# Turning the exponentials and outputs of a local and global attention block on VectorE, with products in 32x32 tiles

## The chip, the cores and the metric

The kernel runs on one core of one Trainium2 chip. The metric is device time in microseconds of one launch. A core has TensorE (matrix products, into PSUM, eight banks of 128 partitions by 512 fp32), VectorE (DVE), ScalarE (ACT), GpSimd (POOL) and a queue engine SP that only issues transfers. Every engine runs its own queue in order and waits on semaphores.

## The reference

Attention over 8 batches and 8 heads of dimension 64, with 512 local and 32 global positions, followed by one wide gated layer, called the mixture of experts (MoE) below.

```python
k_all = np.concatenate([k_g, k_l], axis=2)
s_g = scale * np.matmul(q_g, k_all.transpose(0, 1, 3, 2))
out_g = np.matmul(sm(s_g), v_all)
mask = np.abs(pos[:, None] - pos[None, :]) <= 32
s_ll = np.where(mask, scale * q_l @ k_l.T, -1e9)
s_l = np.concatenate([scale * q_l @ k_g.T, s_ll], axis=-1)
out_l = np.matmul(sm(s_l), np.concatenate([v_g, v_l], axis=2))
x = concatenate([out_g, out_l])        # (4352, 512)
h = x @ w_in                           # (512, 2048)
return (h * np.clip(h + 3, 0, 6) / 6) @ w_out
```

`sm` is a softmax with the row maximum taken off. A local query sees the 32 global keys and local keys at most 32 positions away.

## The kernel before

Positions are cut in 16 blocks of 32. A block of 32 queries sees three blocks of keys (its own and the two beside it) and the 32 global keys, 128 keys in all. A *unit* is one call of `local(b, j, q)`: 128 queries (four blocks) and four of the eight heads, so there are 8 units a batch and 64 in all.

`quad_qk` turns queries and keys on TensorE (L390) and copies them out of PSUM to `qt` and `kt` (L224 on ScalarE, L226 on VectorE). A unit then runs: scores (16 products with 96 local keys, L416, and 16 with 32 global keys, L417); per head, VectorE adds the mask and takes the maximum (L428, written as two instructions); ScalarE takes the exponential into `ex` (L434). `ex` has queries on partitions and must be turned before it can multiply V. For batches 0 to 2 TensorE turns it through PSUM (L446, copied by L224 or L226); for batches 3 to 7 a DMA transpose issued on the SP queue does (L439). Then 16 products with V (L453), one per head and block of queries, each 128 keys by 32 queries, go to the bank `a`, and VectorE divides by the sums (L462, L463) into `x`. `x` is turned again for the MoE: by TensorE for batch 0 (L477), by DMA for the others (L484).

V needs, for each block of queries, its 128 keys on the 128 partitions: the tile `vs` holds one such column of blocks for each of the 16 blocks. It is loaded from memory in part and copied within the chip in part; for batches 0 and 1 TensorE makes it with products with a 0/1 matrix (`pick`, L317), and the global V is spread by GpSimd (L305). `globe` does the 32 global queries of four heads at a time (L501 to L544) and spreads their output over `xg` (L548 to L558).

The MoE: `first` makes 128 hidden features for up to 512 tokens (L582, four products), ScalarE and VectorE apply the gate (L588, L590); `second` makes 128 tokens of the output from 16 products (L601), copied out by L608 or L610 and stored by SP.

The order of each queue is laid beforehand by `Plan.lay`, a list scheduler over named streams with ranks: each `Op` has costs in microseconds per engine, a latency and buffers that it takes and reads. Buffers come from pools of a given size (`sizes`). TensorE's filler is the stream `moe`; attention units of batch b are spread over the MoE of batch b - 1 by `hold`. PSUM is used as: three banks `m` for MoE, two for `s` (two slots of scores), two `t` for turns, one `a`.

Of the kernel before, what the change touches and what calls it, by code (L numbers as in the profile page):

```python
# [13 lines left out]
class Buf:  # L14


    __slots__ = ("pool", "slot", "left", "free_at")

    def __init__(self, pool, readers):
        self.pool, self.slot, self.left, self.free_at = pool, None, readers, 0.0  # L20
# [13 lines left out]
class Plan:  # L34
# [3 lines left out]
    def __init__(self, pools):  # L38
        self.free = {p: [0.0] * n for p, n in pools.items()}
        self.streams = {}  # L40
        self.rank = {}
# [9 lines left out]
    def ready(self, op):  # L51
        t = 0.0
        for d in op.deps:
            if d.end is None:
                return None
            t = max(t, d.end)
        need = {}
        for b in op.takes:
            need[b.pool] = need.get(b.pool, 0) + 1
        for p, n in need.items():  # L60
            slots = sorted(x for x in self.free[p] if x is not None)
            if len(slots) < n:
                return None
            t = max(t, slots[n - 1])
        return t

    def lay(self):
        at = {n: 0 for n in self.streams}
# [3 lines left out]
        while len(order) < total:  # L72
            found = []
            for n, ops in self.streams.items():
# [3 lines left out]
                t = self.ready(op)  # L78
# [12 lines left out]
            if len(op.on) > 1:  # L91
                start, end, e = min((f[0], f[2], f[4]) for f in found if f[3] == n)
                start, end, e = min(((f[0], f[2], f[4]) for f in found if f[3] == n), key=lambda f: f[1])
            at[n] += 1
            clock[e] = end
            op.end, op.engine = end + op.lat, e
            for b in op.takes:
                slots = [(x, i) for i, x in enumerate(self.free[b.pool]) if x is not None]
                b.slot = min(slots)[1]
                self.free[b.pool][b.slot] = None  # L100
            for b in op.reads:
                b.left -= 1
                b.free_at = max(b.free_at, op.end)
                if b.left == 0:
                    self.free[b.pool][b.slot] = b.free_at
# [5 lines left out]
def kernel(  # L111
# [22 lines left out]
    NT = Sl // P  # L134
    W = 32
    NU = P // W
    NB = Sl // W
    NQ = H // 4
    T = 8
    D1 = D + 2  # L140
    NC1 = (NB - 1) // 3
    NS = NB
    PERM = 2
# [12 lines left out]
    def tiles(name, n, shape, dtype, pool=None):  # L156
        return [(pool or sb).tile(shape, dtype, tag=f"{name}{i}", name=f"{name}{i}") for i in range(n)]

    sizes = {"nat": 2, "qkg": 1, "gT": 2, "kt": 2, "v": 2, "ex": 4, "sm": 8, "et": 5, "x": 3, "xt": 3,
             "xgn": 2, "t1": 3, "ot": 3, "m": 3, "s": 2, "t": 2, "a": 1, "eg": 2, "mx": 12, "rec": 4}  # L160
    for c in range(NDFF):
        sizes[f"gts{c}"] = 1

    qn = tiles("qn", 2, [P, NP, T * D], FP16)
    kn = tiles("kn", 2, [P, NP, T * D], FP16)
    qkg = tiles("qkg", 1, [P, H * D], FP16)
    gT = tiles("gT", 2, [P, NQ, 2, P], FP16)
    qt = [tiles(f"qt{r}_", NQ, [P, 2, Sl], FP16) for r in range(2)]
    kt = [tiles(f"kt{r}_", NQ, [P, 2, Sl + 2 * W], FP16) for r in range(2)]
    vs = tiles("vs", 2, [P, NS, H, D1], FP16)  # L170
    vraw = tiles("vraw", PERM, [P, H, NT * D], FP16)
    pick = tiles("pick", 1, [P, NT, Sl + 2 * W], FP16)[0]
    exs = tiles("ex", 4, [P, 4, P], FP16)
    sms = tiles("sm", 8, [P, P], FP32)
    ets = tiles("et", 5, [P, 6 * P], FP16)
    egs = tiles("eg", 2, [P, 6, P], FP16)
    xs = tiles("x", 3, [P, H, D], FP16)
    xts = tiles("xt", 3, [P, NP, Sl], FP16)
    xgns = tiles("xgn", 2, [P, 2, D], FP16)
    xg = tiles("xg", 1, [P, NP, B * Sg], FP16)[0]  # L180
# [3 lines left out]
    recs = tiles("rec", 4, [P, 4, 1], FP32)  # L184
    masks = tiles("mask", 3, [P, P], FP32)
    ident = tiles("ident", 1, [P, P], FP16)[0]
    w_in_t = tiles("win", 4, [P, NP, dff // 4], FP16)
# [4 lines left out]
    mps = tiles("m", 3, [P, 512], FP32, pp)  # L192
    sps = tiles("s", 1, [P, 2 * 512], FP32, pp)[0]
    tps = tiles("t", 2, [P, 1024], FP16, pp)
    aps = tiles("a", 1, [P, 4, D1], FP32, pp)

    plan = Plan(sizes)
    for name, rank in (("l0", 0), ("ld", 5), ("sh", 0), ("et", 0), ("tr", 0), ("st", 2),
                       ("gq", 3), ("gqc", 2), ("qt", 4), ("qtc", 3), ("kg", 1), ("pm", 2), ("pmc", 1), ("vb", 6),
                       ("s", 2), ("mx", 2), ("ex", 2), ("t", 1), ("etc", 2), ("av", 0), ("nm", 1),  # L200
                       ("xp", 1), ("xpc", 1), ("gx", 1), ("gxc", 1),
                       ("moe", 9), ("t1", 0), ("gate", 0), ("ot", 3)):
        plan.stream(name, rank)
    for name in ("l0", "ld", "sh", "et", "tr", "st"):
        plan.stream("dq" + name, 0 if name in ("l0", "ld") else -1)

    def load(stream, engine, issue, service, o, i, deps=(), takes=(), reads=(), transpose=False, lat=2.0):
        eng = {"POOL": nc.gpsimd, "SP": nc.sync}[engine]

        def emit():  # L210
            a, b = o() if callable(o) else o, i() if callable(i) else i
            if transpose:
                eng.dma_start_transpose(out=a, in_=b)
            else:
                eng.dma_start(out=a, in_=b)  # L215
# [17 lines left out]
    BY_DMA = range(3, B)  # L233

    def slot(i):
        return (2 * NC1, 0, NC1)[i % 3] + i // 3

    def setup():
        for r in range(2):
            nc.vector.memset(vs[r][0:W, slot(0), :, :], 0.0)  # L240
            nc.vector.memset(vs[r][2 * W:3 * W, slot(NB - 1), :, :], 0.0)
            nc.vector.memset(vs[r][:, :, :, D:D1], 1.0)
            nc.vector.memset(egs[r], 0.0)
            for q in range(NQ):
                nc.vector.memset(kt[r][q][:, :, 0:W], 0.0)
                nc.vector.memset(kt[r][q][:, :, W + Sl:], 0.0)

    def band():
        m = masks[1]
        nc.vector.memset(m, 0.0)  # L250
# [462 lines left out]
```

## Time and profile before

| | us |
|---|---|
| median of three runs | 400.56 (400.41 to 403.77) |
| the profiled execution | 400.83 |
| its span, first to last instruction | 399.1 |
| granted TensorE clock, mean | 0.987 |

In the profile PE is TensorE, PEld its weight loads, DVE VectorE, ACT ScalarE, POOL GpSimd. A group's line names line, engine, operation, output and inputs, shapes and count, then busy time, mean duration of one in ns, idle time of the engine just before them and what ended it. Products overlap, so their durations are not their pace: the time from one start to the next is.

```profile
L428 DVE CUSTOM_DVE_ANT_0 sm<-s,mask 128x128 f32<-128x128 f32 x256 | 61.8, 285 | 15.6 <-PE s L417 14.7
L453 PE MATMUL a<-vs,et 128*32 128x65 f16 x1024 | 20.1, 198 | 19.5 <-DMA et<-ex 19.5
L463 DVE TENSOR_TENSOR x<-a,rec 128x256 f16<-128x256 f32 x64 | 27.1, 424 | 2.2
```

For instance the last of these: 64 instructions on VectorE of 424 ns, each reading 128 partitions by 256 fp32 from the bank `a`.

### The profile page before, as it was taken

The page shows a single profiled execution, that of the slowest core. Times are in us where ns is not written, and L with a number is a line of the kernel's source. Part 1 is how long each engine was busy: PE and PEld are TensorE (multiplying, and loading weights), DVE is VectorE, ACT ScalarE, POOL GpSimd, SP SyncE. Part 2 cuts the span into 40 slices and gives each one's busy share as a digit, 9 for nine tenths or more (in the row PEclk, how much of TensorE's full clock was granted, in tenths as well). Part 3 has the DMA queues.
Part 4 walks back from the last instruction along what each step waited for, and adds up shares of the span by engine and source line. Part 5 has one row for each costly group of instructions (what it writes and reads, how often), then busy time and mean ns, then how long its engine had stood idle before and what let it go on. Part 6 is the DMA issues. An engine that isn't in the chain of part 4 may idle for free.

```text
span 399.1 us, 13569 instructions
## 1 busy us (share of the span) xinstructions
PE 352.7 (88%) x5604; PEld 181.4 (45%) x5604; DVE 269.5 (68%) x995; ACT 211.9 (53%) x504; POOL 130.4 (33%) x148
## 2 busy tenths in 40 slices
PE   2279899999899988998499987999889989999996
PEld 2245676645444533454234533454334434444562
DVE  5573898687998757876476765876875787457150
ACT  1066778635486456744465563755763576245251
POOL 8953309920880193008900193007400000000000
PEclk9999999999999999999879998999999999999999
DMA  8999929637993199439954299339554442310202
GB/s 109 202 207 207 213 42 113 142 87 151 114 194 58 52 174 206 62 94 120 161 99 102 81 150 206 71 85 119 131 80 107 95 41 53 82 53 2 79 3 79
DMA packets 92942, 44.15 MB, mean 111 GB/s; under 512 B 72176, under 2 KB 86992, under 8 KB 92880
## 3 DMA queue, kind: packets, MB, share of 16 engines
q0 software_dynamic: 48320, 17.77, 40.4%
q1 hardware_dynamic: 44560, 25.51, 31.6%
q8 instruction: 44, 0.72, 0.7%
q14 instruction: 18, 0.15, 0.1%
HBM read 35.52 MB, written 8.91 MB: 111 GB/s over the span
## 4 chain that ended last, share of the span: by engine, by line
PE 59%; DMA 18%; DVE 12%; ACT 4%; POOL 3%; issue 3%; SPq 0%; POOLq 0%; DVEq 0%; ACTq 0%
PE m L601 22%; PE m L582 19%; DMA et<-ex 17%; PE m L317 4%; PE a L453 3%; DVE sm L428 3%; PE s L416 2%; DVE qt L226 2%; ACT ex L434 2%; PE t L390 2%; DVE gts L590 1%; ACT t L588 1%; PE t L523 1%; DVE kt L226 1%; PE t L446 1%
## 5 line engine op out<-in xcount | busy, mean ns | idle before, releaser
L582 PE MATMUL m<-xt,win 128*128 128x512 f16 (+1 forms) x576 | 126.2, 364 | 2.4 <-DVE gts L590 1.8
L434 ACT ACTIVATE ex<-sm,mx 128x128 f16<-128x128 f32 x256 | 88.6, 392 | 65.4 <-DVE mx L428 65.0
L601 PE MATMUL m<-wout,gts 128*128 128x512 f16 x512 | 122.9, 380 | 0.0
L588 ACT ACTIVATE t<-m 128x512 f32<-128x512 f32 (+1 forms) x160 | 84.7, 532 | 44.8 <-PE m L582 38.4
L590 DVE SCALAR_TENSOR_TENSOR gts<-t,m 128x512 f16<-128x512 f32 (+1 forms) x144 | 88.9, 624 | 13.3 <-ACT t L588 12.4
L582 PEld LDWEIGHTS <-win 128*128 128x128 f16 x640 | 58.9, 99 | 54.9 <-issue 8.3
L428 DVE CUSTOM_DVE_ANT_0 sm<-s,mask 128x128 f32<-128x128 f32 x256 | 61.8, 285 | 15.6 <-PE s L417 14.7
L215 POOL DMA_DIRECT2D vs<-in_v_l_dram x42 | 29.8, 716 | 127.2 <-PE a L533 116.9
L601 PEld LDWEIGHTS <-gts 128*128 128x128 f16 x512 | 44.8, 98 | 50.1 <-issue 2.5
L305 POOL COPY vs<-vs 32x2640 f16<-32x2640 f16 x21 | 49.4, 2402 | 0.0
L462 DVE RECIPROCAL rec<-a 128x4 f32<-128x4 f32 x64 | 11.5, 180 | 40.3 <-PE a L453 40.1
L453 PE MATMUL a<-vs,et 128*32 128x65 f16 x1024 | 20.1, 198 | 19.5 <-DMA et<-ex 19.5
L608 ACT COPY ot<-m 128x512 f32<-128x512 f32 x22 | 12.9, 585 | 41.0 <-PE m L601 38.1
L453 PEld LDWEIGHTS <-et 128*32 128x32 f16 x1024 | 12.1, 97 | 45.7 <-DMA et<-ex 27.6
L416 PE MATMUL s<-kt,qt 64*32 64x96 f16 x1024 | 21.7, 211 | 11.3 <-DVE kt L226 6.8
L463 DVE TENSOR_TENSOR x<-a,rec 128x256 f16<-128x256 f32 x64 | 27.1, 424 | 2.2
L416 PEld LDWEIGHTS <-qt 64*32 64x32 f16 x1024 | 13.9, 93 | 19.2 <-issue 11.1
L226 DVE COPY et<-t 128x512 f16<-128x512 f16 (+1 forms) x30 | 14.2, 477 | 12.3 <-PE t L523 9.5
L226 DVE COPY qt<-t 128x1024 f16<-128x1024 f16 x16 | 19.5, 1221 | 2.9 <-PE t L390 2.5
L428 DVE DVE_READ_ACCUMULATOR2_ANT mx<- 128x1 f32 x256 | 21.2, 83 | 0.1
L513 ACT ACTIVATE eg<-s,mx 128x480 f16<-128x480 f32 x16 | 10.6, 661 | 19.3 <-DVE mx L508 17.6
L417 PE MATMUL s<-gT,qt 64*32 64x32 f16 x1024 | 19.5, 180 | 0.0
(73 smaller groups left out, 307.6 us busy)
## 6 DMA issues: line engine op xcount, KB each, us to landing
out_dram<-ot SPq DMA_DIRECT2D x32, 256.0 KB, 2.2
vs<-vs SPq DMA_DIRECT2D x13, 330.0 KB, 4.5
qn<-in_q_l_dram POOLq DMA_DIRECT2D x16, 256.0 KB, 6.7
kn<-in_k_l_dram POOLq DMA_DIRECT2D x16, 256.0 KB, 7.8
vs<-in_v_l_dram POOLq DMA_DIRECT2D x30, 96.0 KB, 4.4
win<-in_moe_w_in_dram POOLq DMA_DIRECT2D x4, 512.0 KB, 13.8
wout<-in_moe_w_out_dram POOLq DMA_DIRECT2D x4, 512.0 KB, 15.3
vs<-vs SPq DMA_DIRECT2D x9, 165.0 KB, 6.5
```

The costliest lines, as they stand in the source:

```text
L215: eng.dma_start(out=a, in_=b)
L226: nc.vector.tensor_copy(out=o(), in_=i())
L305: g.append(plan.add("vb", Op(("POOL", 3.0), lambda dst=dst, src=src: nc.gpsimd.tensor_copy(out=dst(), in_=src()), g[:1])))
L416: nc.tensor.matmul(out=o[:, 0:3 * W], lhsT=lhs, rhs=kt[k.slot][q][rows, e, i * W:(i + 3) * W])
L428: nc.vector.tensor_tensor_reduce(out=sms[sm.slot], in0=sps[:, c0():c0() + P], in1=m, scale=-scale, scalar=3.0e38, op0=ALU.add, op1=ALU.min ...
L434: nc.scalar.activation(out=exs[ex.slot][:, h, :], in_=sms[sm.slot], func=EXP, scale=-1.0, bias=mxs[mx.slot])
L453: nc.tensor.matmul(out=aps[0][u * W:(u + 1) * W, h, 0:D + 1], lhsT=ets[et.slot][:, h * P + u * W:h * P + (u + 1) * W], rhs=vs[v.slot][:, s ...
L463: nc.vector.tensor_tensor(out=xs[x.slot][:, 4 * q:4 * q + 4, :], in0=aps[0][:, :, 0:D], in1=recs[rec.slot].to_broadcast([P, 4, D]), op=ALU ...
L582: nc.tensor.matmul(out=mps[ps.slot][:, 0:n], lhsT=w_in_t[c // 4][:, m, (c % 4) * P:(c % 4 + 1) * P], rhs=x[:, m, :], start=(m == 0), stop= ...
L588: r = plan.add("t1", Op(("ACT", 0.14 + n * 0.00083), lambda: nc.scalar.activation(out=t1s[t1.slot][:, 0:n], in_=mps[ps.slot][:, 0:n], func ...
L590: return plan.add("gate", Op(("DVE", 0.12 + n * 0.00104), lambda: nc.vector.scalar_tensor_tensor(out=gfn(), in0=t1s[t1.slot][:, 0:n], scal ...
L601: nc.tensor.matmul(out=mps[ps.slot], lhsT=gfn(c), rhs=w_out_t[c // 4][:, c % 4, :], start=(c == 0), stop=(c == NDFF - 1))
```

## The change

A unit becomes `local(b, j)`: 128 queries and all eight heads, 32 units in all. The keys are kept in one line, `kt`, in which a block of global keys stands before every four local blocks, so that the four blocks of 32 keys that a block of queries sees are 128 neighbouring columns. One product of 128 columns replaces the two of 96 and 32. The order of the four (previous block m, own 0, next p, global g) differs with the block of queries (`ORDER`, `FROM`). GpSimd inserts the global keys into the line (`insert`).

VectorE turns the exponentials in 32x32 blocks of 32-bit words, each word two exponentials (`tt`). After that the 32 keys of one block lie on 32 partitions, and each product with V is 32 keys by 32 queries, 128 products a unit, added up over the four blocks in PSUM. The V of the previous and of the next block must lie on the same partitions: `vm` and `vp` are copies of `v0` shifted by 32 positions, made by DMA on the SP queue, and `v4` is the global V four times (GpSimd). The products write four banks, one per block of queries. VectorE divides (one pair of instructions for eight heads) and turns the output in 32x32 blocks (`tx`, and for the global queries the last `gn`); the feature order that this gives is matched by reading W_in with its rows in that order.

No product with `pick`, no transpose by DMA and no turn of `ex` or `x` by TensorE is left; the global queries' exponentials are still turned by TensorE. PSUM is now: two banks `m`, four banks `a`, of which two (`am`) also serve the MoE and two (`t`) also serve turns and global queries, and one slot of scores of two banks. The products with V take all four banks of `a`; the planner's new `claims` keeps other streams from taking `am` and `t` while that step is ready.

```diff
-             "xgn": 2, "t1": 3, "ot": 3, "m": 3, "s": 2, "t": 2, "a": 1, "eg": 2, "mx": 12, "rec": 4}
+    sizes = {"nat": 2, "qkg": 2, "gT": 2, "kt": 2, "v": 2, "ex": 2, "sm": 8, "et": 2, "x": 2, "xt": 3,
+             "eg": 2, "etg": 2, "xgn": 2, "t1": 3, "ot": 3, "m": 2, "am": 2, "t": 2, "s": 1, "mx": 12, "rec": 2}
...
+    def slots(self, pool, name):
+        for n, pools in self.claims.items():
+            if n != name and pool in pools and self.at[n] < len(self.streams[n]):
+                if all(d.end is not None for d in self.streams[n][self.at[n]].deps):
+                    return []
+        return [(x, i) for i, x in enumerate(self.free[pool]) if x is not None]
...
+    plan = Plan(sizes, {"av": ("am", "t")})
...
+        for u in range(1, NU):
+            spread.append(plan.add("vg", Op(("POOL", 0.7), lambda u=u: nc.gpsimd.tensor_copy(
+                out=v4[v.slot][u * W:(u + 1) * W], in_=v4[v.slot][0:W]), [g])))
...
+            shift(lambda j0=j0, j1=j1: vp[v.slot][0:P - W, j0:j1], lambda j0=j0, j1=j1: v0[v.slot][W:P, j0:j1], deps, 0.45 * n, range(j0, j1))
+            shift(lambda j0=j0, j1=j1: vm[v.slot][W:P, j0:j1], lambda j0=j0, j1=j1: v0[v.slot][0:P - W, j0:j1], deps, 0.45 * n, range(j0, j1))
...
+            def insert(q=q):
+                line = kt[k.slot][q][:, :, W:LINE - W].rearrange("d e (a c) -> d e a c", c=W)
+                for e in range(2):
+                    nc.gpsimd.tensor_copy(out=line[:, e, 0:5 * NJ + 1:5, :],
+                                          in_=gT[g.slot][:, q, e:e + 1, Sg:].to_broadcast([P, NJ + 1, Sg]))
...
-                        nc.tensor.matmul(out=o[:, 0:3 * W], lhsT=lhs, rhs=kt[k.slot][q][rows, e, i * W:(i + 3) * W])
-                        nc.tensor.matmul(out=o[:, 3 * W:P], lhsT=lhs, rhs=gT[g.slot][rows, q, e, gc:gc + Sg])
+                            rows, i, c0 = slice(r * D, (r + 1) * D), NU * j + u, (5 * j + FROM[u]) * W
+                            nc.tensor.matmul(out=sps[u * W:(u + 1) * W, at(2 * q + r, e):at(2 * q + r, e) + P],
+                                             lhsT=qt[k.slot][q][rows, e, i * W:(i + 1) * W],
+                                             rhs=kt[k.slot][q][rows, e, c0:c0 + P])
...
+            def turn(e=e):
+                nc.vector.transpose(out=ets[et.slot][:, e].rearrange("p c k -> p (c k)").bitcast(FP32),
+                                    in_=exs[ex.slot][:, e].rearrange("p c k -> p (c k)").bitcast(FP32))
+            turned.append(plan.add("tt", Op(("DVE", 0.33), turn, exps, [et] if e == 0 else (), [ex])))
+        held = [Buf("am", 1), Buf("am", 1), Buf("t", 1), Buf("t", 1)]
...
+                for n, src in (("m", vm), ("0", v0), ("p", vp), ("g", v4)):
+                    for u in range(NU):
+                        w = ORDER[u].index(n)
+                        a, bb = w // 2, w % 2
+                        rows = slice(u * W, (u + 1) * W)
+                        for c in range(NC):
+                            lhs = ets[et.slot][rows, e, c, :].rearrange("p (a q b) -> p a q b", a=2, b=2)[:, a, :, bb]
+                            h = 2 * c + e
+                            rhs = v4[v.slot][rows, h, 0:D + 1] if n == "g" else src[v.slot][rows, j, h, 0:D + 1]
+                            nc.tensor.matmul(out=aps[c * W:(c + 1) * W, u, e * (D + 1):(e + 1) * (D + 1)], lhsT=lhs, rhs=rhs,
+                                             start=(n == "m"), stop=(n == "g"))
...
+        n = plan.add("nm", Op(("DVE", 0.9), normal, [a], [rec, x], held + [rec]))
...
+            nc.vector.transpose(out=xts[xt.slot][:, :, j * P:(j + 1) * P].rearrange("p k (u t) -> p k u t", u=NU),
+                                in_=xs[x.slot].rearrange("p u (r k) -> p k u r", k=KC))
...
-        ps, t1 = Buf("m", 1), Buf("t1", 1)
+        ps, t1 = Buf(("m", "am"), 1), Buf("t1", 1)
...
-            at = b - 1 + (i - LEAD) / (NQ * NJ + 2)
+            at = b - 1 + (i - LEAD) / 10
```

## The prediction

> **What bounds the kernel now.** I read the busy table first, then the chain that ended last, then the waits, then a table of busy time cut at the starts of the batches, and last the shapes of the groups on TensorE.
>
> ```profile
> PE 352.7 (88%) x5604; PEld 181.4 (45%) x5604; DVE 269.5 (68%) x995; ACT 211.9 (53%) x504; POOL 130.4 (33%) x148
> PE 59%; DMA 18%; DVE 12%; ACT 4%; POOL 3%; issue 3%; SPq 0%; POOLq 0%; DVEq 0%; ACTq 0%
> PE m L601 22%; PE m L582 19%; DMA et<-ex 17%; PE m L317 4%; PE a L453 3%; DVE sm L428 3%; PE s L416 2%; DVE qt L226 2%; ACT ex L434 2%; PE t L390 2%; DVE gts L590 1%; ACT t L588 1%; PE t L523 1%; DVE kt L226 1%; PE t L446 1%
> ```
>
> TensorE carries the chain, and the one large thing on it that is no computation is the DMA transpose of the exponentials (17% of 399.1 us). The waits say what of that is idle TensorE:
>
> ```profile
> PE a L453 <- DMA et<-ex: 19.5, 14, 4.1
> PE s L416 <- DVE kt L226: 6.8, 1, 6.8
> ```
>
> The timeline of TensorE has the first L582 of the batches at 40.1, 104.3, 146.3, 187.5, 234.5, 277.5, 315.6 and 352.6 us. The busy time between these:
>
> ```profile
> 0.00:40.10 40.10, 22.66 (x437) 14.33 (x438) 21.64 (x83) 14.64 (x34) 26.77 (x47) 1.00 1.15 182
> 40.10:104.30 64.20, 60.24 (x1279) 39.03 (x1279) 53.65 (x224) 41.68 (x114) 30.44 (x30) 1.00 0.83 121
> ...
> 187.50:234.50 47.00, 40.75 (x663) 18.91 (x662) 30.49 (x117) 24.60 (x58) 17.04 (x19) 0.93 0.87 116
> ...
> 315.60:352.60 37.00, 34.54 (x495) 15.61 (x494) 25.09 (x94) 19.44 (x46) 0.00 (x0) 1.00 0.37 69
> 352.60:399.00 46.40, 42.47 (x225) 21.70 (x223) 17.70 (x32) 19.69 (x39) 0.00 (x0) 1.00 0.12 40
> ```
>
> Columns after the length: TensorE, weight load, VectorE, ScalarE, GpSimd, clock, DMA. So there are four stages: a start of 40.1 us with TensorE idle for 17; a first batch of 64.2 us, in which VectorE is busy 84%; six windows that sum to 248.3 us (41.4 each), the worst, at 47.0, with 6 us idle and a granted clock of 0.93; a tail of 46.4 us, mixture of experts (MoE) alone. A full MoE of one batch is 64 L582 and 64 L601; in the tail 64 L582 start over 13.8 us, 0.216 each, so 128 x 0.216 = 27.6 us. No window can be shorter than that plus the attention that shares it.
>
> **The change, part by part.** Attention on TensorE, per batch. *Scores:* 32 products of one unit start at 245.74 us, the next L582 at 246.02: 0.28 us. The first of the 32 starts at 245.742, the last at 245.911, so 5.5 ns apart. After, 32 products of 128 columns make a whole unit of eight heads; I take 0.33, 4 units: 1.3 us, where before 8 x 0.28 = 2.2. *Products with V:* 16 products (128 rows, 32 columns) take 245.50 to 245.74, 15 ns each. After there are 128 of 32x32 per unit. No row shows that shape. Lower end: the 4 ns median from start to start inside the L453 groups, 0.5 us plus 0.12 for the change of shape. Upper end inside the case: 15 ns, 1.97 us. I take the 6 ns of the score group, the nearest for narrow rows: 128 x 6 + 120 = 0.89 us, 3.6 per batch (0.62 to 1.97 give 2.5 to 7.9), where before 8 x 0.24 = 1.9. *Query and key turns* stay (0.58 x 4) with 0.4 for the global ones: 2.8. *Global queries* 2.0 (16 groups of scores 5.8, turns 6.7, values 5.1 over eight batches, with five blocks for six). Sum 1.3 + 3.6 + 2.8 + 2.0 = 9.7, with MoE 37.3 us.
>
> The Trainium skill ("TensorE: Matmul & The Clock Gate", Back-to-back issue gap) says that start to start never drops below about 25 ns however small the product. By that rule a unit would take 3.2 us. The trace contradicts it for the narrow shapes it has (4 to 6 ns).
>
> VectorE, per batch, by start-to-start times of dense stretches: gates 16 x 0.605 = 9.7; L428 32 x 0.211 = 6.8; normalisation 4 x (0.21 + 0.61), the 512 columns priced as a gate, 3.3 (before 8 x 0.55 = 4.4); globals 2.6; a quarter of the query and key copies, the rest of which stands on ScalarE in the built order, 1.1; copies of outputs and global turns 2.2. New are the turns: 8 of 128x256 words and 4 of 128x512 halves. The nearest rows are L463 (256 columns in 0.34) and L590 (512 in 0.605): 8 x 0.34 + 4 x 0.6 = 5.1. The far row is the copy of 128 columns at L259 in 0.661 us, beside a busy GpSimd: 5.2 ns a column, 1.32 and 2.64, together 21. I take 5.1, as L463, L590 and the 384-word memset (0.378) all say about one column a cycle. Sum 30.8 us, 78% of a 39.5 us window: it feeds, it does not set the pace. ScalarE: 32 x 0.292 + 16 x 0.494 + 3 x 0.95 + 3 = 23 us; hidden.
>
> Removed from the waits: the 40 transposes of L439 and the 28 of L484, issued on the SP queue. What is late next is VectorE: the products with V now wait for its turns, and they take four banks at once (two of the pool am, two of t) until L462 and L463 have read them: 0.9 + 0.25 + 0.83 + 0.2 = 2.2 us, in which MoE has the two banks m. One first-layer group needs 0.866 + 0.25 + 0.5 + 0.6 + 0.2 = 2.4 us of a bank, 1.2 us per group by two banks where TensorE needs 0.866: 0.33 lost per group, two groups per hold, with some 1.7 of the four holds in the first layer: 1.1 us. The other 1.1 is for other waits (the idle of the calmest window, 37.0 - 34.5 = 2.5, holds both kinds). Window: 37.3 + 2.2 = 39.5 us, 6 x 39.5 = 237. The single score slot (two banks, freed by eight L428) costs nothing while units come 6 us apart, as eight take 1.7 us; without that cover it is 1.7 us a unit.
>
> Start. TensorE's first turn ends at 6.3 us, the last operand at 12.3; then L416 waits 6.8 us for VectorE, which stood 4.6 us behind the mask's GpSimd work and 2.8 us in its copies. After, the mask is two small selections issued at 3 us, and 23 copies of 32 columns (about 0.1 each, as the memset of 0.085) that end before the key copies. Scores start near 13.6; units of 2.4 us on ScalarE (8 x 0.292) and 2.4 to 3.8 on VectorE give two units' outputs by about 22. The shifted copies of V (loads issued near 10, 4.4 us to land, then a copy of 4.5 as the vs<-vs row) come by 20 to 22, the first quarter of W_in (issued near 14 behind GpSimd's insertion of the global keys into the line, that is 5 us later than now, 13.8 to land by the median) by 22 to 28. First L582 at 25, between 22 and 34. The 76 products L317 (18 us) and their copies are gone.
>
> First batch. MoE 27.8, rest of its own attention 3.8, next batch's turns, scores and global scores 4.8: 36.4. In the built order its four groups of products with V for batch 1 stand behind one another after the last L601 of batch 0, and the next MoE waits for them: 4 x 2.2 + 0.6 = 9.4. With 4 for other waits 50 us, between 45 and 62. V of batch 1 has to be there at 65 us; now it lands near 47.
>
> DMA otherwise: shifted copies of 1.1 MB a batch replace the copies vs<-vs (5.8 MB in all) and the element-wise transposes; the SP queue puts them ahead of output stores, which have three buffers. Hidden at a DMA share of 0.4 to 1.0, else a store of 2.2 us is late. GpSimd loses 49 us of L305. Output and tail stay: 46.4.
>
> Sum: 25 + 50 + 237 + 46.4 = 358.4 us of span, and 1.7 for what lies around it (400.83 against 399.1): 360. The profiled execution is 0.3 us above the median shown, so the same holds against 400.56.
>
> **The rivals.**
> *Forecast* (0.55): as above, 350 to 372 from the ends of window and start.
> *Narrow products do not overlap* (0.06; slower): place, the 4096 products with V. Each 10 ns over the 6 taken costs 41 us as TensorE sets the pace; from 16 ns on the change is slower. At the 29 ns median from start to start of the turns L390, where few products overlap, it is 360 + 94 = 454. Against it stand the 4 to 6 ns of the narrow groups; for it, that no row has 32 rows. The floor of the Trainium skill's page above, 25 ns, would give 438.
> *VectorE becomes the bound* (0.11): at 1.32 and 2.64 us a turn VectorE has 46.7 us a batch: windows of 48, first batch 58, sum 25 + 58 + 288 + 48 = 419. It decides from 39.5 us a batch; half the surcharge gives 39, windows of 42, about 375. Half of this chance lies below 397.
> *Waits move rather than vanish* (0.16): the four-bank hold and the in-order TensorE queue cost what the DMA did, windows stay at 41.4 to 44; only start and first batch gain: 25 + 52 + 6 x 43 + 48 = 383.
> *The start stays* (0.10): V in 128-byte rows lands late, GpSimd's queue being blocked by the insertions; first batch ends at 93 instead of 75: 378.
> *The change does not do what it says* (0.02): nothing here; the built order has the turns and no DMA transposes.
>
> **How the numbers follow.** Predicted 360, the likeliest case. Range 344 to 390: down to windows of 37.3 with a start of 22, up past the third and fourth rivals; what is left out is the first rival, the worst half of the second and some of the unseen. Faster by over 1% (about what this kernel's measurement tells from no change): 0.55 + 0.16 + 0.10 + 0.06 = 0.87. Slower: 0.06 + 0.03 = 0.09; the remaining 0.04 within 1%.
>
> **What would show it.** Right: no DMA on the chain, first L582 near 25, the second batch's near 75, windows of 38 to 41; a unit with V in 0.7 to 1.0 us; a turn of 256 words at 0.34 to 0.45 us; VectorE busy about 31 us a window. Wrong: a unit with V above 2 us, TensorE waiting for the turns for over 3 us a window, VectorE above 90%, or an output store or shifted copy on the chain.

## The result and the profile after

The changed kernel takes 481.9 us (median of 4 runs, 480.1 to 484.6) where the kernel before takes 402.2 on the same chip (4 runs, 400.4 to 403.9). The ratio is 1.199 with a 95% interval of 1.190 to 1.208: a fifth slower, where 360 us was forecast. The profiled execution has a span of 480.3 us.

The busy table and the chain of the page of after:

```profile
PE 362.7 (76%) x7408; PEld 193.2 (40%) x7408; DVE 262.2 (55%) x981; ACT 215.7 (45%) x493; POOL 95.1 (20%) x160
PE 57%; DVE 17%; ACT 11%; issue 8%; DMA 4%; POOL 2%; SPq 1%; ACTq 0%; POOLq 0%; DVEq 0%
PE m L590 21%; PE a L572 13%; PE a L478 8%; DVE gts L579 8%; ACT t L577 7%; PE m L572 5%; PE a L408 4%; ACT kt L247 2%; DVE x L486 2%; ACT qt L247 2%; DMA vp<-v 2%; PE s L436 2%; DMA qkg<-in_k_g_dram 2%; PE a L533 1%; DVE sm L450 1%
```

The DMA transpose that held 17% of the chain is gone, as the change says. TensorE is busy for 362.7 us, 10 more than before, in a span that is 81 us longer, so nearly all of the loss is idle TensorE. VectorE is busy 55% of the span and is not the bound. But the gate of the first layer (L579) and its relu (L577) now stand on the chain with 15%; before, the lines for them (L590, L588) had 2%. "issue", time in which an engine waits for nothing that the profile shows, had 3% before and has 8%.

The waits on TensorE (line, what released it, us in total, times, longest):

```profile
PE a L572 <- DVE gts L579: 15.4, 15, 1.8
PE a L478 <- issue: 13.3, 9, 5.1
PE a L408 <- ACT kt L247: 5.1, 4, 1.8
PE a L408 <- ACT t L577: 2.8, 3, 1.6
```

The third and fourth are the odd ones. A turn of queries or keys (L408) has a bank of its own, yet here it waits for ScalarE to copy the turn before it out of the other of the two banks `t`, or to finish the relu of a first-layer group in a bank `am`. The timeline of after shows such a chain, 125 to 132 us (start, length, engine, line, and in brackets the idle time before and what ended it):

```profile
124.96 0.64 PE L408 MATMUL a<-ident,qn 128*64 128x128 f16 x16 [0.45 <-DVE gT L249]
...
125.64 0.60 ACT L577 ACTIVATE t<-a 128x512 f32<-128x512 f32 x1 [2.28 <-PE a L408]
...
126.28 0.64 PE L408 MATMUL a<-ident,kn 128*64 128x128 f16 x16 [0.69 <-ACT t L577]
...
128.00 0.69 DVE L579 SCALAR_TENSOR_TENSOR gts<-t,a 128x512 f16<-128x512 f32 x1 [2.50 <-ACT qt L247]
...
128.74 1.67 PE L572 MATMUL a<-xt,win 128*128 128x512 f16 x4 [1.82 <-DVE gts L579]
...
131.51 1.07 PE L408 MATMUL a<-ident,qn 128*64 128x128 f16 x16 [1.10 <-ACT kt L247]
```

Read it downwards. Sixteen turns write one bank, the relu of another bank starts when they end, the next turns start when the relu ends, a gate waits for the copy of a turn, the next first-layer product waits for that gate. In this stretch the banks of `a` are served strictly one after another. The list of waits has the same for the relu, which eight times waits for a turn into another bank:

```profile
ACT t L577 <- PE a L408: 14.1, 8, 2.6
```

The four banks are one tile, `aps`. The suspicion is that its accesses keep the order of the program whichever bank they touch; the first two experiments test it.

The tail, where no attention is left, shows it alone:

```profile
427.67 1.89 PE L572 MATMUL m<-xt,win 128*128 128x512 f16 x8
430.60 1.89 PE L572 MATMUL a<-xt,win 128*128 128x512 f16 x8 [1.03 <-DVE gts L579]
432.32 1.89 PE L572 MATMUL m<-xt,win 128*128 128x512 f16 x8
435.24 1.89 PE L572 MATMUL a<-xt,win 128*128 128x512 f16 x8 [1.03 <-DVE gts L579]
```

In these rows the groups in the tiles `m` follow on, and each pair in `a` waits 1.03 us for a gate of the pair before. The tail takes 54.4 us where before it took 46.5.

Cut at the first L572 of each batch, the busy time by stage (columns as in the table of before):

```profile
0.00:33.90 33.90, 9.85 (x456) 7.95 (x457) 19.51 (x123) 13.59 (x34) 21.21 (x39) 1.00 1.21 170
33.90:118.40 84.50, 57.05 (x1252) 35.96 (x1252) 39.64 (x144) 29.56 (x77) 21.67 (x33) 0.82 0.69 105
118.40:182.40 64.00, 49.04 (x983) 24.75 (x981) 31.73 (x115) 28.17 (x59) 12.16 (x22) 0.89 0.37 57
...
387.80:425.90 38.10, 35.39 (x643) 16.93 (x642) 25.64 (x90) 20.92 (x47) 0.00 (x0) 1.00 0.08 30
```

The first batch has 27 us in which TensorE does nothing. There the other kind of idle time stands. The products with V of the second batch, 512 of them in a row from 103.1 us, take 12.98 us from the first start to the last; most later units, standing alone, take 1.01 to 1.04 for 128. Inside the row the engine stops six times, in turn for two reasons: three times for the normalisation of the unit before (3.95 us together), and three times, exactly 128 products apart, where it waits for no other engine ("issue", 3.68 us). The waits of the whole first batch have both:

```profile
PE a L478 <- issue: 9.3, 5, 5.1
PE a L478 <- DVE x L486: 3.9, 3, 1.5
```

The instructions themselves come by a DMA queue, which the third part of the page lists (packets, MB, share of 16 engines), first before, then after:

```profile
q8 instruction: 44, 0.72, 0.7%
```

```profile
q8 instruction: 58, 0.95, 0.8%
```

A packet is 16 KB. 58 packets for twice 7408 instructions on TensorE, 44 for twice 5604: one packet for every 128 pairs of weight load and product. A unit with V has just as many instructions as one packet holds. Around the 512 products the packets start at 104.8, 109.8, 113.1 and 116.8 us. All 12 stops on TensorE's products that are marked "issue" (the shortest 0.38 us) end 2.2 to 3.0 us after the start of such a packet, and the packets come one in about 8 us on the mean.

So there were two theories. **A:** the one tile of four banks. **B:** the supply of instructions to the short products. The rival to both was C, that the hold of four banks itself, or the streaming of the narrow products, costs the time.

### The profile page after: what moved, and what is told of

Same layout as the page of the kernel before. It is cut to its first block, busy times and chain, and to the rows that moved or that the text cites. A ratio compares the mean times of both kernels' runs of the same rounds, so it can differ in the third digit from the quotient of the medians.

```text
span 480.3 us, 16949 instructions
## 1 busy us (share of the span) xinstructions
PE 362.7 (76%) x7408; PEld 193.2 (40%) x7408; DVE 262.2 (55%) x981; ACT 215.7 (45%) x493; POOL 95.1 (20%) x160
## 3 DMA queue, kind: packets, MB, share of 16 engines
q1 hardware_dynamic: 8192, 17.03, 11.1%
## 4 chain that ended last, share of the span: by engine, by line
PE 57%; DVE 17%; ACT 11%; issue 8%; DMA 4%; POOL 2%; SPq 1%; ACTq 0%; POOLq 0%; DVEq 0%
PE m L590 21%; PE a L572 13%; PE a L478 8%; DVE gts L579 8%; ACT t L577 7%; PE m L572 5%; PE a L408 4%; ACT kt L247 2%; DVE x L486 2%; ACT qt L247 2%; DMA vp<-v 2%; PE s L436 2%; DMA qkg<-in_k_g_dram 2%; PE a L533 1%; DVE sm L450 1%
## 5 line engine op out<-in xcount | busy, mean ns | idle before, releaser
L590 PE MATMUL m<-wout,gts 128*128 128x512 f16 x512 | 121.8, 382 | 1.6 <-DVE gts L579 1.6
L572 PEld LDWEIGHTS <-win 128*128 128x128 f16 x640 | 63.3, 104 | 101.1 <-issue 54.2
L572 PE MATMUL a<-xt,win 128*128 128x512 f16 (+1 forms) x268 | 63.2, 372 | 31.2 <-DVE gts L579 15.4
L572 PE MATMUL m<-xt,win 128*128 128x512 f16 (+1 forms) x308 | 76.8, 392 | 6.7 <-issue 3.1
L579 DVE SCALAR_TENSOR_TENSOR gts<-t,a 128x512 f16<-128x512 f32 (+1 forms) x67 | 41.5, 630 | 70.7 <-ACT t L577 46.7
L577 ACT ACTIVATE t<-a 128x512 f32<-128x512 f32 (+1 forms) x75 | 39.0, 533 | 80.2 <-PE a L572 47.0
L590 PEld LDWEIGHTS <-gts 128*128 128x128 f16 x512 | 46.1, 98 | 54.9 <-issue 5.0
L577 ACT ACTIVATE t<-m 128x512 f32<-128x512 f32 (+1 forms) x85 | 44.0, 533 | 44.8 <-PE m L572 42.0
L478 PEld LDWEIGHTS <-et 32*32 32x32 f16 x4096 | 36.0, 90 | 42.4 <-issue 40.1
L579 DVE SCALAR_TENSOR_TENSOR gts<-t,m 128x512 f16<-128x512 f32 (+1 forms) x77 | 46.2, 613 | 8.4 <-ACT t L577 8.4
L478 PE MATMUL a<-v,et 32*32 32x65 f16 x2048 | 37.7, 206 | 12.5 <-issue 12.4
L390 POOL COPY kt<-gT 128x160 f16<-128x160 f16 x32 | 8.8, 321 | 131.2 <-DVE gT L249 97.7
L462 DVE STREAM_TRANSPOSE et<-ex 128x256 f32<-128x256 f32 x64 | 28.1, 439 | 9.6 <-ACT ex L456 7.3
L478 PE MATMUL a<-vm,et 32*32 32x65 f16 x1024 | 19.3, 206 | 12.8 <-DVE gts L579 4.8
L238 POOL DMA_DIRECT2D v<-in_v_l_dram x32 | 28.2, 895 | 2.0 <-DMA wout<-in_moe_w_out_dram 1.6
```

The costliest lines, as they stand in the source:

```text
L238: eng.dma_start(out=o() if callable(o) else o, in_=i() if callable(i) else i)
L462: nc.vector.transpose(out=ets[et.slot][:, e].rearrange("p c k -> p (c k)").bitcast(FP32), in_=exs[ex.slot][:, e].rearrange("p c k -> p (c ...
L478: nc.tensor.matmul(out=aps[c * W:(c + 1) * W, u, e * (D + 1):(e + 1) * (D + 1)], lhsT=lhs, rhs=rhs, start=(n == "m"), stop=(n == "g"))
L572: nc.tensor.matmul(out=bank(ps)[:, 0:n], lhsT=w_in_t[c // 4][:, m, (c % 4) * P:(c % 4 + 1) * P], rhs=x[:, m, :], start=(m == 0), stop=(m = ...
L577: r = plan.add("t1", Op(("ACT", 0.14 + n * 0.00083), lambda: nc.scalar.activation(out=t1s[t1.slot][:, 0:n], in_=bank(ps)[:, 0:n], func=REL ...
L579: return plan.add("gate", Op(("DVE", 0.12 + n * 0.00104), lambda: nc.vector.scalar_tensor_tensor(out=gfn(), in0=t1s[t1.slot][:, 0:n], scal ...
```

## The experiments

**four_tiles.** The four banks become four tiles; the normalisation, which one instruction could read from one tile, becomes four reciprocals and four products. The order of the queues stays.

```diff
-    aps = tiles("a", 1, [P, NU, 512], FP32, pp)[0]
+    aps = tiles("a", NU, [P, 512], FP32, pp)
...
-        return mps[b.slot] if b.at == "m" else aps[:, b.slot, :]
+        return mps[b.slot] if b.at == "m" else aps[b.slot]
...
+            for u in range(NU):
+                o = aps[u][:, 0:2 * (D + 1)].rearrange("p (e d) -> p e d", e=2)
+                nc.vector.reciprocal(out=recs[rec.slot][:, u, :], in_=o[:, :, D])
```

> The changed kernel with its four banks as four tiles instead of one tile of four banks. The order of every queue stays; what differs is which waits the program carries, and that VectorE divides a unit in four pairs of instructions instead of one (some 0.7 us more a unit). Theory A (the four banks, being one tile, are kept in program order among one another, so that the relu of one bank waits for a turn into another): the MoE alone in the tail, 54.1 us in the changed kernel with 1.4 us holes, goes back to 46 to 49 us, the holes at turns and copies go, and the whole gains 50 to 80 us, to 400 to 430. Theory B (the products with V come faster than TensorE's instructions are brought in, and that sets the pace): 465 to 482, tail as it was. Theory C (the hold of four banks at once starves the MoE): 470 to 490, since the hold gets longer.

398.4 us (395.4 to 402.7), ratio to before 0.989, interval 0.984 to 0.994. That is just past the 400 to 430 expected. So A holds: 83 us of the 482 go with the declaration of a tile, although VectorE has 192 instructions more. C is out as the cause of these 83 us, since the hold gets longer and the narrow products are the same. The waits of the first layer (L575 here) for gates and of the turns for relu are gone from TensorE's list; what leads it now is

```profile
PE a L478 <- issue: 15.1, 10, 4.3
PE a L379 <- DMA qkg<-in_k_g_dram: 7.9, 1, 7.9
PE s L436 <- DVE mx L450: 5.3, 2, 3.4
PE a L478 <- DMA vm<-v: 3.7, 1, 3.7
```

**before_one_tile.** The reverse, in the kernel before: its three banks `m` as one tile.

```diff
-    mps = tiles("m", 3, [P, 512], FP32, pp)
+    mps = tiles("m", 1, [P, 3, 512], FP32, pp)[0]
```

> The kernel before with its three banks m as one tile of three banks, nothing else. Theory A: the first layer loses its overlap between banks, 0.5 to 1.5 us for each of some 144 groups, and the kernel takes 460 to 600 us, far above its 400. Theories B and C: no change, 400 to 404.

696.4 us (one execution), more than any theory said, and for A. Its waits on TensorE are the same kind as in after, and longer:

```profile
PE m L582 <- ACT t L588: 109.1, 78, 2.6
PE m L582 <- DVE gts L590: 34.5, 35, 2.0
```

Not all of it is waiting: TensorE's busy time grows from 352.7 to 469.7 us for the same instructions, at a granted clock of 0.752 where the kernel before has 0.987. That is most likely a consequence of the idle time, but no run shows it apart.

**half_products.** four_tiles with the products over the blocks "0" and "p" left out, and with them their part of the result: 64 a unit.

```diff
-                for n, src in (("m", vm), ("0", v0), ("p", vp), ("g", v4)):
+                for n, src in (("m", vm), ("g", v4)):
```

> Four tiles as in four_tiles, and of each unit's 128 products with V the 64 over the own and the next block are left out, so the outputs lack these keys; all else stays. At 8 ns a product this takes 0.5 us of TensorE a unit, 16 us in all, if TensorE sets the pace. Theory A alone: 0 to 16 us below four_tiles. If theory B holds beside A (256 instructions a unit have to be brought in, and TensorE stands inside the unit meanwhile): 20 to 45 us below four_tiles, and the holes of 1 us and more inside the products with V are gone.

365.2 us (one execution), 33 less: 16 ns for each product left out, twice the 8 ns from start to start of a unit that runs free. From the first product's start to the last's, the units with V sum to 55.5 us in four_tiles and to 22.7 here; the difference of 32.8 is the whole gain. About half of it is 64 products fewer at 8 ns (16.4 us); the stops marked "issue" before these products, 15.1 us in four_tiles, fall to 1.2. That says where the time is, not yet whether it is supply or streaming.

**narrow_columns.** All 128 products kept, but those same 64 write 8 columns instead of 65.

```diff
-                            nc.tensor.matmul(out=aps[u][c * W:(c + 1) * W, e * (D + 1):(e + 1) * (D + 1)], lhsT=lhs, rhs=rhs,
-                                             start=(n == "m"), stop=(n == "g"))
+                            wide_n = 8 if n in "0p" else D + 1
+                            nc.tensor.matmul(out=aps[u][c * W:(c + 1) * W, e * (D + 1):e * (D + 1) + wide_n], lhsT=lhs,
+                                             rhs=rhs[:, 0:wide_n], start=(n == "m"), stop=(n == "g"))
```

> The kernel of four_tiles with its 128 products with V a unit kept, but those over the key blocks '0' and 'p' write 8 columns instead of 65 (the part of the result that they would add to the other columns is left out). half_products, without these 64 products, took 365.2 us where four_tiles took 398.4. Theory B (the supply of instructions: one 16 KB packet for every 128 weight loads and products): the count is that of four_tiles, so the time stays at 393 to 402 us, with holes of 2 to 4 us marked 'issue' in the line of the products. Rival (the array's streaming time: 64 products of 57 columns fewer): most of the 33 us comes back, 365 to 378 us. An even split would be near 382.

397.5 us (one execution): nothing comes back. It is the number of instructions and not the columns. A lone unit still takes 1.02 us, the row of 512 still 13.2.

**double_products.** Every product with V issued twice into the same sum.

```diff
-                                             start=(n == "m"), stop=(n == "g"))
+                            for twice in range(2):
...
+                                                 start=(n == "m" and twice == 0), stop=(n == "g" and twice == 1))
```

> The kernel of four_tiles with every product with V issued twice in a row into the same sum (numerator and denominator both double, so the quotient stays): 256 a unit, 4096 more in all. Theory B: a stretch of these goes at the 26 to 28 ns for each pair of weight load and product that 512 pairs back to back took in four_tiles (80 to 95 us), part of it beside other work as before: the 2048 pairs that half_products left out gave 16 ns each, so 4096 more cost 66 to 110 us, 464 to 508 us, with 90 packets of instructions instead of 58. Rival (streaming alone, 4 to 8 ns from start to start): 16 to 33 us more, 414 to 431 us.

557.5 us (one execution), 90 packets. That is 159 us for 4096 pairs, 39 ns each, and more than I expected. No unit runs freely now: the shortest takes 2.6 us, where 256 pairs at 8 ns would take 2.0. The stops marked "issue" on TensorE's products go from 19.3 us in four_tiles to 97.6, and 4096 products at 8 ns are 33 more; what makes up the other 49 us of the 160 that the span grows was not taken apart. The timeline of the long row (now 1024 products, from 99.3 to 127.1 us):

```profile
100.67 0.45 PE L479 MATMUL a<-v,et 32*32 32x65 f16 x28
103.58 0.23 PE L479 MATMUL a<-v,et 32*32 32x65 f16 x2 [2.46 <-issue]
...
105.42 0.86 PE L479 MATMUL a<-vm,et 32*32 32x65 f16 x29 [0.98 <-DVE x L490]
...
108.13 0.24 PE L479 MATMUL a<-v,et 32*32 32x65 f16 x2 [1.53 <-issue]
```

Stops marked "issue" come inside a unit, while VectorE has little or nothing to do, and behind the 188th, the 316th and the 444th product of the row, and so on: all seven exactly 128 apart. The rows of after, four_tiles and narrow_columns stop behind the same 188th, 316th and 444th product. From 105.7 us on the packets start every 3.5 to 3.8 us there. So this stretch goes no faster than 128 pairs in about 3.6 us, 28 ns a pair. And each of the 45 stops of this run that are marked so ends 2.2 to 3.3 us after a packet starts, before whichever line it stands; in four_tiles the 12 end 2.2 to 3.1 us after one, while its waits of over 0.4 us for other engines or transfers end anywhere from 0.3 to 20 us after one. The stops end with the packets. The row as a whole:

```profile
99.30:127.20 27.90, 12.97 (x1025) 10.75 (x1024) 7.37 (x32) 1.20 (x2) 0.00 (x0) 0.55 0.17 50
```

TensorE is idle for more than half of it, and VectorE, the busiest of the others, works 7.4 of 27.9 us. The 0.98 us for L490 is the hold: the next unit's products may not write the banks before they are normalised. It is one stop a unit, about 1 us, the smaller part.

**no_shifted_copies.** four_tiles with `v0` read in place of `vm` and `vp`, and no copies of V by DMA.

```diff
-                for n, src in (("m", vm), ("0", v0), ("p", vp), ("g", v4)):
+                for n, src in (("m", v0), ("0", v0), ("p", v0), ("g", v4)):
```

> The kernel of four_tiles without the two shifted copies of V (the products over the blocks 'm' and 'p' read the copy of block '0', so their part of the result is that of other keys); 9 MB of transfers go, the number of instructions on TensorE stays. If the copies matter (the one wait of 3.7 us for vm, and packets of instructions that stand behind bulk transfers in the first 45 us, where they come every 6 us), 385 to 394 us; theory B with a supply that does not depend on the bulk transfers: 395 to 400 us, the 512 products back to back still at 26 to 28 ns each.

397.9 us: the copies, without which queue q1 moves 8.1 MB less (8.92 for 17.03), cost nothing that can be told, though the wait for vm is gone. (The planner, with V usable earlier, also pulled the second batch's units apart; all 32 units sum to 55.7 us, against 55.5 in four_tiles, so that gave nothing either.)

**pairs_of_banks** and **pairs_of_banks_2.** The products of a unit as two steps of 64 with two banks each.

```diff
+        for half_u in range(2):
+            held = [Buf("am", 1), Buf("am", 1)] if half_u == 0 else [Buf("t", 1), Buf("t", 1)]
+            us = range(2 * half_u, 2 * half_u + 2)
```

> The kernel of four_tiles with the products with V of a unit issued as two steps of 64, each for two query blocks and two banks, with its own normalisation, laid as two operations by the planner; same instructions in number, another order. Theory B: where the planner puts other products between the two halves the supply catches up, holes marked 'issue' in the line of the products fall from 27 us to 10 to 20, and the hold of two banks for four leaves the mixture of experts more: 380 to 394 us. Against it: the stretch of 512 products of the second batch stays one stretch in this order and its 13 us with it. If neither supply nor hold matters, 396 to 401 us.

428.3 us. It does not count for the question: the planner's buffer of V was given back after half of its reads, so the next batch's V was loaded too early, parts of the result come from it, and products waited for those loads. With that put right:

> pairs_of_banks with the buffers of V kept until both halves of every unit have read them (there they were given back after half the reads, so the next batch's V was loaded over them early and the global products waited 7 us for it in steps of 0.82). The stretch of 512 products of the second batch stays. Theory B, by the runs so far: a unit that starts with its instructions in place takes 1.02 us, a stretch beyond what is in place 26 ns a pair; halves that stand apart cost 0.48 each. 385 to 398 us; if the hold of four banks matters to the mixture of experts beside this, the low end. If neither matters, 396 to 401 us.

404.7 us, ratio 1.005 (0.999 to 1.010): no gain from holding two banks instead of four, and not the 385 to 398 expected. The planner's order changed with it, so the total is no clean measure of the hold. The row of 512 products is a better one: its order is the same but for the halves. No stop in it is put down to the normalisation any more, where four_tiles had 2.6 us, but those marked "issue" grow from 4.0 to 7.3 us, and the row takes 13.1 us for 13.6. So in this row the hold hides behind the supply. Where the supply does not limit, the hold shows: in half_products, with no "issue" left in the row, its three stops are 2.9 us of a row of 7.0.

**spaced_units, spaced_early_v, four_tiles_early_v, before_early_v.** If short products in a row cost 28 ns a pair and alone 8, an order that spreads them should help. A pause in the planner's model behind each unit, and the second batch's V loaded before W_out:

```diff
+        supply.append(plan.add("ff", Op(("FETCH", 2.4), lambda: None, [a], lat=0.0)))
...
-        w_out_l = load_w_out()
         v_loads(1, "ld")
+        w_out_l = load_w_out()
```

> four_tiles with the planner told of the supply: behind each unit's products with V a pause of 2.4 us before the next unit's, 1.05 us for the unit itself and 1.6 for the normalisation. Only the order of the queues changes; 384 of the second batch's 512 products still stand in one stretch, as its V arrives late. Theory B: 390 to 398 us (the later units are apart already at 1.02 us each). If the order does not matter: 396 to 401 us.

401.5 us (one execution).

> spaced_units with the loads of the second batch's V issued before those of W_out, so the planner puts its four units apart, inside the first batch's mixture of experts. Theory B: the stretch that took 13.6 us in four_tiles and the half clock behind it (0.50 to 0.59 from 84 to 100 us) go: 12 to 18 us of the 398.4, so 380 to 388 us, with units of 1.0 to 2.5 us there. If the total of instructions is what limits (58 packets at 3.5 us, 203 us, far below the span) or W_out now comes late, 392 to 402 us.

395.9 us (392.7 to 399.7), ratio 0.979 (0.969 to 0.989).

> The kernel before with one edit: the loads of the second batch's V are issued before those of W_out. A control for spaced_early_v: if that kernel's gain over four_tiles comes from the order of the loads alone, the kernel before gains 3 to 10 us as well (391 to 398 us). If it comes from pulling the second batch's dense products apart (the kernel before has 16 larger products a unit and no such stretch), the kernel before stays at 399 to 406 us, or loses a little as W_out lands later.

398.5 us, ratio 0.995 (0.990 to 1.000).

> four_tiles with the same edit of the loads and no model of the supply in the planner: of the second batch's four units two stand back to back (256 products), two alone, where spaced_early_v has all four apart and four_tiles all in one stretch of 512. Theory B at 26 ns a pair: some 5 to 9 us below four_tiles, 389 to 394 us. If the gain needs the planner's spacing: 396 to 402 us.

401.3 us, ratio 0.998 (0.993 to 1.004). What theory B was expected to give here did not come in any of the three: spaced_units is just above the 396 to 401 of an order that does not matter, spaced_early_v in the 392 to 402 of its rival, four_tiles_early_v in the 396 to 402 of its rival, and the control lies between its two ranges. The long row did go: in spaced_early_v the second batch's four units take 1.4, 1.9, 1.5 and 1.0 us. But the summed stops of TensorE, of whatever cause, above 0.7 us from one product's start to the next are 42.0 us in four_tiles and 43.9 in spaced_early_v. They moved into the scores and the first layer, which stand behind the units in the same queue:

```profile
PEld L479 <- issue: 26.7, 34, 4.7
PEld L437 <- issue: 19.0, 26, 3.4
...
PEld L577 <- issue: 11.4, 6, 5.1
```

Here L437 is the scores and L577 the first layer; in four_tiles the same three had 34.1, 15.6 and 8.5 us. spaced_early_v is the fastest complete version, 1 to 3% below the kernel before, but its interval overlaps that of four_tiles, so the spacing is not shown to bring anything of its own.

## Why the prediction was wrong

By stage, from the starts of the batches in each profiled execution:

| us | forecast | before | after | four_tiles | half_products |
|---|---|---|---|---|---|
| start | 25 | 40.1 | 33.9 | 30.1 | 28.6 |
| first batch | 50 | 64.2 | 84.5 | 66.6 | 55.0 |
| six windows | 237 | 248.3 | 307.5 | 251.9 | 233.1 |
| tail | 46.4 | 46.5 | 54.4 | 46.6 | 46.6 |
| span | 358.4 | 399.1 | 480.3 | 395.2 | 363.3 |

With four tiles and half of the short products left out the kernel comes within 5 us of the forecast. That is no confirmation: the forecast had counted the other half too.

*The stalls of 2.2 us a window* failed, and this is the step that turned the sign. I priced the step that takes four banks as a hold of 2.2 us and 1.1 us of lost first layer, as if each bank were waited for by itself. They are one tile, so a use of one bank waits for the earlier uses of the other three, in first-layer groups, turns and global products, whether or not a unit holds the banks. The six windows lost 307.5 - 251.9 = 55.6 us to that, with whatever lower clock the stops brought along, the first batch 17.9, the tail 7.8, the start 3.8. The hold, which I did price, has no such cost: it stands in four_tiles too, and halved in pairs_of_banks_2 it brought no gain. The line that says it was in the code shown, the write to `aps[c * W:(c + 1) * W, u, ...]`: one name with a bank index, where before each bank had a tile.

*The tail stays* failed by the same cause. I took for granted that an untouched stage keeps its time, but half of its groups had been moved into the tile `a`.

*A unit with V in 0.89 us* was near for one that finds its instructions fetched (1.02 us, 8 ns a product for 6 assumed). As a sum it was wrong: 32 x 0.89 = 28.5 us, measured 55.5 in four_tiles. Of these, 32 times 1.02 is 32.6, stops marked "issue" are 15.1, and one wait of the first unit for the shifted copy `vm` is 3.7; the other 4 were not taken apart. I costed the products by their time in the array and never by what it takes to bring 256 instructions. The sign was there to read: the page before lists 44 packets of 16 KB, and 5604 pairs shared over them is 128, just the number that a unit now has. Of the 37 us of span between forecast and four_tiles the units make 27.

*The first batch* (50) had both: its row of four units was forecast at 9.4 us including holds, and took 13 to 13.6 with 512 products in every kernel that kept it. It also had a term at nothing that none of the theories named, the clock. I took 0.216 us for each MoE product throughout; in four_tiles the granted clock is 0.50 from 15.5 to 49.6 us and from 83.7 to 100.8, and before 49 us first-layer products of 256 columns start 0.213 us apart where later ones take 0.109. Summed over the MoE products at half clock, I estimate about 6 us of four_tiles for this (3 in the first batch) and 10 of after.

*The start* came out at 33.9, inside the 22 to 34 given, and 30.1 without A. What was missing in the 25 is mostly not supply: until 30.1 us four_tiles has one stop marked "issue", of 0.5 us, but waits of 3.7 us for the first shifted copy, 5.3 for the maxima of the scores in their single slot and 2.1 for the turned outputs. The supply follows in the first batch: at 38.8 and 44.7 us stops of 3.1 and 4.3 us end, while packets come about every 6 us beside transfers of 167 to 233 GB/s.

*The turns on VectorE* were right. Their groups in after (count, then busy time in all and ns of one, then idle time before them):

```profile
L462 DVE STREAM_TRANSPOSE et<-ex 128x256 f32<-128x256 f32 x64 | 28.1, 439 | 9.6 <-ACT ex L456 7.3
L494 DVE STREAM_TRANSPOSE xt<-x 128x512 f16<-128x512 f16 x32 | 22.2, 693 | 0.3
```

Their ends overlap the next instruction: in four_tiles, where others follow at once, they take 0.36 us (forecast 0.34) and 0.59 to 0.63 (0.60) from start to start. VectorE is busy 26 to 34 us a window there, about the 31 forecast. The rival that made VectorE the bound rightly had a small chance. That narrow products overlap was right too. (The rival of products that do not overlap took 29 ns from the turns L390; the median in the trace of before is 26.) The Trainium skill ("TensorE: Matmul & The Clock Gate", Back-to-back issue gap) gives about 25 ns as the floor from start to start for 1 to 64 columns; the lone unit's 8 ns with 65 columns, and the median of 3 ns with 128 in the scores, all products in parts of the array, do not keep to it. The 28 ns of a long stretch resembles it in size, but the stops come in one piece every 128 pairs and not between all products, so it is another thing.

*The shifted copies are hidden* was right for the total: leaving them out changed nothing. It was not right for the first unit, which in after waits 1.9 us for vm and 2.4 for vp; "DMA vp<-v 2%" stands on the chain, which the prediction had named as a sign of being wrong. The last window of after, 38.1 us, hit the forecast of 39.5, yet four_tiles needs 34.8 for it; it agreed by chance.

Of the rivals, "waits move rather than vanish" named hold and in-order queue and priced them at 383. The mechanism behind the 482 was neither; it was not among the rivals.

Not settled: why a packet takes about 3.6 us to come round when it occupies its queue for about 1 us, and how many instructions can lie ready. No run changed either, so B rests on the number of products, on the steps of 128 and on the times of the packets. How much a kernel with four tiles and fewer, larger products would gain was tried only by leaving products out.

## What to carry to other kernels

Before costing a change that merges buffers, ask what the unit of waiting is. In this program a tile of several PSUM banks is waited for as one thing: splitting it back gave 83 us here, and merging three banks of the tuned kernel cost it 295 in the one execution taken. Count instructions as well as array time: here 128 short products and their weight loads ran at 8 ns each when they lay ready and at 28 in a long row. A low mean is no safety: four_tiles has 58 packets in 395 us, one in 6.8, and still 19 us of such stops. And an order that moved the short products apart did not help here: as many stops came elsewhere.

## What the hardware showed beyond that

The granted clock halves without a long idle stretch. In four_tiles, windows of 2 us around the row of short products (columns as above, the clock third from the end):

```profile
80.00:82.00 2.00, 2.00 (x132) 1.32 (x131) 1.28 (x3) 1.05 (x2) 0.00 (x0) 1.00 0.32 112
82.00:84.00 2.00, 0.98 (x60) 0.57 (x50) 1.85 (x11) 0.15 (x1) 0.00 (x0) 0.93 0.39 133
84.00:86.00 2.00, 1.11 (x96) 0.82 (x84) 0.93 (x3) 0.00 (x0) 0.00 (x0) 0.50 0.63 188
...
98.00:100.00 2.00, 2.00 (x44) 0.91 (x43) 0.83 (x3) 0.60 (x1) 0.00 (x0) 0.50 0.00 0
100.00:102.00 2.00, 2.00 (x15) 0.74 (x14) 1.23 (x6) 0.60 (x1) 1.81 (x3) 0.80 0.30 25
```

By 84 us the clock is at 0.50, when the longest stop from one product's start to the next had been 1.2 us; of the 3.4 us before its fall TensorE had been busy for 2.4. In after, half_products and narrow_columns it falls as well, 2.8 to 5.4 us into this row. In four_tiles it stays there until TensorE has been fully busy from about 96 to 101 us. The Trainium skill ("TensorE: Matmul & The Clock Gate", What's actually happening) has the clock fall after an idle window of about 3.4 us and return after about as long a busy one; the return agrees with these rows, the fall came here without such an idle time in the trace.
